# A new order for the first quarter of a hand-written work list and of the list of loads

## The chip, the cores and the metric

The kernel runs on one core of one Trainium2 chip. The metric is the device time of one execution in microseconds: 364.95 us, the median of three runs before the change (364.71 to 365.18).

## The reference, cut to what matters

Causal attention with 16 extra "beacon" keys that every query sees, then a gated feed-forward block on its output:

```python
# q, k, v: 8 batches, 8 heads, 576 rows, 64 columns;  beacon_k, beacon_v: 16 rows
k_all = concat([beacon_k, k]);  v_all = concat([beacon_v, v])
scores = q @ k_all.T / 8, causal mask on the 576 ordinary keys
a = softmax(scores);  attn = a @ v_all
x = attn.transpose(0, 2, 1, 3).reshape(4608, 512)
g = x @ w_gate                      # 512 to 1536
out = (g * sigmoid(g) * (x @ w_val)) @ w_out
```

All inputs are float32 in memory; the kernel casts them to bf16 in the load.

## The kernel before, in words

**Attention.** Heads are worked in pairs, 4 pairs to a batch. Queries and keys have to be turned (head dimension onto partitions) first: of batch 0 in five turns from the loaded runs, of batches 1 and 2 one turn to a pair (`turn`, letter T) after the two heads were laid side by side by `pair_up` (g on VectorE, f on GpSimd), of batches 3 to 7 by DMA transposes (t). `turned_copy` brings them to SBUF (K and Q on VectorE, k and q on ScalarE). A pair's scores are four units A to D (`scores`: S, or s with the mask added by matmuls; letters below such as "scores 2.1B" are batch 2, pair 1, unit B), each with one exponent (`exponent`, E, ScalarE) and for S a mask after it (D on VectorE, M on GpSimd). The product with v has two halves (`pv`, P and p) and a division (`normalize`, R). In batch 0 the first 240 queries of all pairs go ahead: `pv_front` (Z), `normalize_front` (N), `x_turn_front` (J), `x_copy_front` (I); the rest of its rows are turned by X and copied by y. Later batches use DMA transposes (V).

**Feed-forward.** 9 chunks of 512 tokens by 12 column tiles. `gate_value` has two halves (G, H), `tanh` (a, ScalarE) and two VectorE steps (1, 2) follow; `project` (F) is one twelfth of half an output tile, O and o evacuate and store. Chunk 0 starts with its first 240 tokens, so the first gate product waits only for the front rows of batch 0.

**Weights in two shapes.** Scores, turns of batch 1 and 2, gate, value and projection use 64 rows of the array at a time, two such products side by side. `pv` of batches 0 to 3, `pv_front` and the x turns use all 128 rows.

**PSUM.** There are 4 slots of two banks for everything (`take`, `give`): a unit that takes a slot waits for the step that gave that slot back. Slots go round in program order.

**The order.** Every engine works in the order in which the letters of `plan` stand. Each letter l starts the next load of `order_of_loads`, on GpSimd's queue. The first 24 of them are free; each later one waits for the last but one PE step placed before it (line 739, "paced load"). GpSimd has eight completion semaphores for its loads, so a load also waits until the load eight places before it has landed. Names of loads: K0.0 and Q0.4 are keys and queries of batch 0, heads 0 to 3 or 4 to 7; K1, Q2 are a whole batch; v0.0 is the beacons of v, v0.1 to v0.5 are blocks of rows of v of batch 0 (block by block of 128 keys); g0 to g4 and u0 to u4 are column parts of w_gate and w_val (1, 2, 3, 3 and 3 tiles); b1, b2 are beacon keys; o0, o1 are the halves of w_out; k3.1 is a block of rows of k of batch 3.

**Warmers.** Letter h makes the next scores, pv or pv_front issue two more 64 x 128 matmuls of the identity before its own, into the slot that it then overwrites (`keep_warm`, line 182).

Of the kernel before, what the change touches and what calls it, by code (L numbers as in the profile page):

```python
# [16 lines left out]
S = 576  # L17
D = 64
# [68 lines left out]
def kernel(  # L87
# [579 lines left out]
    def select_below():  # L667
        for row in range(2):
            r = slice(HALF * row, HALF * row + HALF)
            nc.gpsimd.affine_select(  # L670
                out=below[r], in_=below[r], compare_op=ALU.is_ge, fill=-30000.0, base=0,
                pattern=[[HALF, 2], [-1, P]], channel_multiplier=1,
            )

    def select_upper():
        nc.gpsimd.affine_select(
            out=upper[:], in_=upper[:], compare_op=ALU.is_ge, fill=0.0, base=0, pattern=[[1, P + NB]],
            channel_multiplier=-1,
        )
# [38 lines left out]
        named[f"K0.{h}"] = lambda h=h: runs(0, k, h, h + 4, FRONT, ROWS)  # L718
        named[f"Q0.{h}"] = lambda h=h: runs(0, q, h, h + 4, FRONT, ROWS)
    order_of_loads = """  # L720
    K0.0 Q0.0 v0.2 Q0.4 K0.4 v0.1 v0.0 v0.3 v0.4 v0.5 g1 u0 g0 u1 g2 u2 K1 Q1 b1 u3 g3 g4 u4 Q2 v1.5 K2 v1.3 v1.2
    v1.0 v1.1 v1.4 b2 o0 o1 v2.2 k3.0 v2.1 q3.2 v2.5 k3.5 v2.4 v2.3 v2.0 q3.4 q3.0 q4.2 k4.0 v3.3 k3.1 q4.0 k3.4
    k3.2 q3.1 v3.0 k4.2 q3.3 k4.3 v3.5 q4.4 k3.3 v3.4 v3.2 k4.5 k4.1 q4.3 q4.1 v4.1 v4.5 v4.3 v4.0 k4.4 v3.1 v4.2
    q6.1 k5.0 q5.1 q5.4 k5.3 k5.5 k6.0 k5.2 k5.1 q5.0 k6.2 q5.3 v4.4 k6.1 q6.0 q6.2 k6.5 q5.2 v5.2 k5.4 k7.0 k7.2
    v5.5 q7.1 k6.3 k7.1 v5.1 q7.2 k7.4 q7.3 q6.3 v5.4 k6.4 q6.4 k7.5 v5.0 k7.3 v5.3 q7.4 q7.0 v6.0 v6.1 v6.2 v6.4
    v6.3 v6.5 v7.4 v7.5 v7.2 v7.1 v7.3 v7.0
    """
    loads = [named[name] for name in order_of_loads.split()]
    assert sorted(order_of_loads.split()) == sorted(named)
    turns = [load for b in range(NPE, B) for load in dma_transposes(b)]  # L730

    def piece(kind):
        as_kind = {"s": "S", "M": "D", "k": "K", "q": "Q", "Y": "y", "o": "O", "i": "I", "A": "e", "f": "g"}.get(kind, kind)
        n = done.get(as_kind, 0)
        done[as_kind] = n + 1
        if kind == "l":
            if n >= FREE_LOADS:

                after(nc.gpsimd.nop(), passed[-2], "paced load")
            loads[n]()  # L740
        elif kind == "b":
            cast_beacons()
        elif kind == "W":
            first_beacon_turn()
        elif kind in "Ae":
            first_beacon_copy(nc.vector if kind == "A" else nc.scalar)
        elif kind == "0":
            regroup()
        elif kind in "gf":
            pair_up(n, nc.vector if kind == "g" else nc.gpsimd)  # L750
        elif kind == "B":
            select_below()
        elif kind == "U":
            select_upper()
        elif kind == "T":
            turn(n)
        elif kind in "KkQq":
            turned_copy(n, kind in "Kk", nc.vector if kind in "KQ" else nc.scalar)
        elif kind in "Ss":
            scores(n, kind == "s")  # L760
        elif kind == "E":
            exponent(n)
        elif kind in "DM":
            while shown[n + skipped[0]][1]:
                skipped[0] += 1
            mask(n + skipped[0], nc.vector if kind == "D" else nc.gpsimd)
        elif kind in "Pp":
            pv(n, kind == "p")
        elif kind == "R":
            normalize(n)  # L770
        elif kind == "X":
            x_turn(n)
        elif kind in "Yy":
            x_copy(n, nc.vector if kind == "Y" else nc.scalar)
        elif kind == "V":
            x_transpose(n + 1)
        elif kind == "t":
            turns[n]()
        elif kind in "GH":
            gate_value(n, kind == "H")  # L780
        elif kind == "Z":
            pv_front(n)
        elif kind == "N":
            normalize_front(n)
        elif kind == "J":
            x_turn_front(n)
        elif kind in "Ii":
# [39 lines left out]
    for kind in "".join(plan.split()):  # L827
# [8 lines left out]
        S=16 * B, E=16 * B, P=NP, p=NP, R=NP, X=NPAIR, y=NPAIR, V=B - 1, t=len(turns), G=NU, H=NU, Z=2, N=2, J=2, I=2, a=NU, **{"0": 1, "b": 1, "W": 1, "e": 1, "g": NPAIR * (NPE - 1), "B": 1, "U": 1, "1": NU, "2": NU}, F=2 * NF * 2 * NCH, O=4 * NCH + 2, T=len(TURNS),  # L836
        K=len(COPIES), Q=len(COPIES),  l=len(loads),
# [31 lines left out]
```

## Time and profile before

| | us |
|---|---|
| median of three runs | 364.95 |
| span of the profiled execution, first to last instruction | 362.0 |
| the rest of the median, outside that span | 2.95 |
| PE busy in the span | 352.9 (97%) |
| VectorE, ScalarE, GpSimd busy | 225.4, 187.6, 124.6 |

PE means TensorE matmuls, POOL is GpSimd, DVE is VectorE, ACT is ScalarE. The trace has the start and length of every instruction, what ended the idle time before it, and when each load landed. A busy PE is not always a PE at its full rate, since the ends of pipelined matmuls are modelled: a matmul of 128 rows by 65 columns is shown with 0.19 us while the next one starts 0.03 us later.

### The profile page before, as it was taken

What the parts mean: (1) busy time and instruction counts of PE and PEld (TensorE: products, weight loads), DVE (VectorE), ACT (ScalarE), POOL (GpSimd) and SP (SyncE); (2) the same over time, 40 slices, a digit from 0 to 9 for tenths busy, and PEclk for the clock granted to TensorE, in tenths of its full rate; (3) what the DMA queues carried; (4) which work ended last, traced back from release to release, by engine and by line L of the source; (5) the groups of instructions that cost most, each with busy time, mean ns of one, the idle gap of its engine ahead of it and who ended that gap; (6) DMA issues with size and microseconds to landing.
All of it is one profiled execution on the core that took longest, in us unless ns stands there. A gap on an engine that the chain in (4) does not pass through costs nothing.

```text
span 362.0 us, 11888 instructions
## 1 busy us (share of the span) xinstructions
PE 352.9 (97%) x5160; PEld 198.6 (55%) x5160; DVE 225.4 (62%) x439; ACT 187.6 (52%) x284; POOL 124.6 (34%) x188
## 2 busy tenths in 40 slices
PE   7799999999999999999999999999999999999996
PEld 3587565654444566554565566546655554455544
DVE  5577997566766654487528754776467764464342
ACT  4966999723434777544863576447633232221310
POOL 8945499926247545374423013111000000000000
PEclk9999999999999999999999999999999999999999
DMA  8999999999999999999979829502413000110113
GB/s 121 156 197 204 191 191 158 174 175 147 149 147 121 134 136 129 153 174 135 122 132 147 109 37 154 67 6 26 113 62 65 2 2 0 61 60 1 61 60 116
DMA packets 146132, 39.74 MB, mean 110 GB/s; under 512 B 131488, under 2 KB 141728, under 8 KB 146080
## 3 DMA queue, kind: packets, MB, share of 16 engines
q0 software_dynamic: 97424, 19.00, 72.1%
q1 hardware_dynamic: 48368, 19.79, 27.9%
q8 instruction: 40, 0.66, 0.8%
q10 hardware_dynamic: 288, 0.20, 0.2%
q14 instruction: 12, 0.10, 0.1%
HBM read 38.27 MB, written 9.44 MB: 132 GB/s over the span
## 4 chain that ended last, share of the span: by engine, by line
PE 85%; DMA 5%; POOL 5%; DVE 2%; ACT 1%; issue 1%; POOLq 0%
PE gv_ps L168 49%; PE o_ps L168 25%; DMA qk<-in_q_dram 5%; PE s_ps L168 5%; PE pv_ps L168 4%; PE pv_ps L493 2%; POOL qk L209 2%; POOL vb L219 1%; DVE x L522 1%; POOL wg L248 1%; POOL wv L248 1%; DVE p L414 1%; PE t_ps L166 0%; ACT p L405 0%; ACT th L579 0%
## 5 line engine op out<-in xcount | busy, mean ns | idle before, releaser
L168 PE MATMUL gv_ps<-xT,wv 64*128 64x512 bf16 (+2 forms) x912 | 203.2, 365 | 0.0
L168 PE MATMUL gv_ps<-xT,wg 64*128 64x512 bf16 (+2 forms) x912 | 202.8, 365 | 0.1
L579 ACT ACTIVATE th<-gv_ps 128x512 f32<-128x512 f32 (+2 forms) x114 | 65.4, 575 | 116.5 <-PE gv_ps L168 116.1
L405 ACT ACTIVATE p<-s_ps 128x832 bf16<-128x832 f32 (+2 forms) x127 | 104.3, 868 | 32.4 <-PE s_ps L168 28.7
L168 PE MATMUL o_ps<-wo,hT 64*128 64x512 bf16 (+2 forms) x912 | 116.5, 365 | 0.2
L584 DVE SCALAR_TENSOR_TENSOR u<-th,gv_ps 128x512 f32<-128x512 f32 (+2 forms) x114 | 74.7, 656 | 65.9 <-ACT th L579 65.1
L168 PEld LDWEIGHTS <-wg 64*128 64x128 bf16 x912 | 82.5, 94 | 45.9 <-PE gv_ps L168 2.4
L168 PEld LDWEIGHTS <-wv 64*128 64x128 bf16 x912 | 81.8, 94 | 40.1 <-issue 0.7
L591 DVE SCALAR_TENSOR_TENSOR hT<-gv_ps,u 128x512 bf16<-128x512 f32 (+2 forms) x114 | 74.7, 661 | 3.0
L168 PEld LDWEIGHTS <-hT 64*128 64x128 bf16 x912 | 42.3, 94 | 34.1 <-PE o_ps L168 1.2
L219 POOL DMA_DIRECT2D vb<-in_v_dram x40 | 33.9, 853 | 64.1 <-PE s_ps L168 25.7
L168 PE MATMUL s_ps<-qT,kT 64*128 64x336 bf16 (+3 forms) x512 | 43.0, 250 | 1.9 <-ACT kT L256 1.0
L168 PEld LDWEIGHTS <-kT 64*128 64x128 bf16 x512 | 23.8, 94 | 22.9 <-ACT kT L256 1.8
L219 POOL DMA_DIRECT2D qk<-in_q_dram x25 | 21.2, 851 | 25.7 <-PE gv_ps L168 7.1
L414 DVE TENSOR_TENSOR p<-p,upper 128x256 bf16<-128x256 bf16 (+2 forms) x84 | 24.0, 317 | 9.8 <-ACT p L405 8.1
L522 DVE TENSOR_TENSOR x<-pv_ps,rec 128x640 bf16<-128x640 f32 (+1 forms) x32 | 25.3, 791 | 1.2
L521 DVE RECIPROCAL rec<-pv_ps 128x10 f32<-128x10 f32 (+1 forms) x32 | 6.8, 213 | 28.1 <-PE pv_ps L168 22.7
L258 DVE COPY o_sb<-o_ps 128x512 f32<-128x512 f32 (+2 forms) x20 | 12.7, 654 | 17.0 <-PE o_ps L168 13.9
L219 POOL DMA_DIRECT2D qk<-in_k_dram x25 | 21.3, 856 | 5.4 <-PE gv_ps L168 4.3
L418 POOL TENSOR_SCALAR_AFFINE_SELECT p<-p 128x256 bf16<-128x256 bf16 (+2 forms) x46 | 17.4, 399 | 14.0 <-ACT p L405 13.8
L168 PEld LDWEIGHTS <-p 64*128 64x128 bf16 x960 | 18.8, 94 | 4.5 <-PE pv_ps L168 0.2
L168 PE MATMUL pv_ps<-vb,p 64*128 64x65 bf16 x960 | 19.9, 189 | 0.0
(65 smaller groups left out, 141.4 us busy)
## 6 DMA issues: line engine op xcount, KB each, us to landing
out_dram<-o_sb SPq DMA_DIRECT2D x34, 256.0 KB, 2.6
vb<-in_v_dram POOLq DMA_DIRECT2D x24, 128.0 KB, 5.7
qk<-in_q_dram POOLq DMA_DIRECT2D x21, 128.0 KB, 5.6
qk<-in_k_dram POOLq DMA_DIRECT2D x16, 128.0 KB, 5.9
wo<-in_moe_w_out_dram POOLq DMA_DIRECT2D x2, 768.0 KB, 10.1
wg<-in_moe_w_gate_dram POOLq DMA_DIRECT2D x3, 384.0 KB, 11.7
wv<-in_moe_w_val_dram POOLq DMA_DIRECT2D x3, 384.0 KB, 14.2
qk<-in_k_dram POOLq DMA_DIRECT2D x2, 576.0 KB, 11.5
```

The lines of the kernel that those rows point to most:

```text
L168: ins = nc.tensor.matmul(o, lhsT=l, rhs=r, start=start, stop=stop)
L209: return nc.gpsimd.dma_start(qk[b % 2][base : base + HALF, RUN * h0 : RUN * h1] .rearrange("p (h e) -> p h e", e=RUN)[:, :, D * i0 : D * i ...
L219: return nc.gpsimd.dma_start(dst[p0 : p0 + n, c, :, 0:D], src[b, :, r : r + n, :].rearrange("h j d -> j h d"))
L248: nc.gpsimd.dma_start(t[:, :, cols], src[:, cols].rearrange("(kk p) f -> p kk f", p=P))
L258: eng.tensor_copy(o, i)
L405: nc.scalar.activation(p_of(b, m, u == "A")[:, :, c0 : c0 + w], ps[:, :, 0:w], ACT.Exp, scale=0.125)
L414: nc.vector.tensor_tensor(out=ap, in0=ap, in1=upper[:, None, d : d + w].to_broadcast([P, 2, w]), op=ALU.mult)
L418: nc.gpsimd.affine_select(out=ap, in_=ap, compare_op=ALU.is_ge, fill=0.0, base=d, pattern=[[0, 2], [1, w]], channel_multiplier=-1,)
L522: nc.vector.tensor_tensor(out=xs[b][:, c0:NKT, P * m : P * m + P].rearrange("p c (h d) -> p h c d", d=D), in0=o[:, :, :, 0:D], in1=rec[:, ...
L579: nc.scalar.activation(th[:, 0:w], gvs[n][:, 0, 0:w], ACT.Tanh, scale=0.5)
L584: nc.vector.scalar_tensor_tensor(out=u[:, 0:w], in0=ths[n][:, 0:w], scalar=1.0, in1=gvs[n][:, 0, 0:w], op0=ALU.add, op1=ALU.mult)
L591: nc.vector.scalar_tensor_tensor(out=hTs[j][:, f, c0:c1], in0=gvs.pop(n)[:, 1, 0 : c1 - c0], scalar=0.5, in1=ths.pop(n)[:, 0 : c1 - c0], o ...
```

## The change

Three things are done. The first 708 of the 1756 letters of the plan stand in a new order, and the first 59 of the 125 loads. The rule for pacing is spelled by letter: L is a free load, l a paced one; there are again 24 free loads, but the 23rd (v1.3) is paced and the 28th (Q2) is free. Five of the ten warmers move from the first stretch to the end of the new part, just before half p of pv 3.1; they are issued by the next P, of pv 3.2. Nothing is added or removed.

The set of the first 16 loads is the same, as is that of the first 32; K1 and Q1 stay number 17 and 18, o0 and o1 number 33 and 34. Within the first 16, u1 goes ahead of all of v0 but v0.2, and g0 ahead of v0.5.

```diff
     order_of_loads = """
-    K0.0 Q0.0 v0.2 Q0.4 K0.4 v0.1 v0.0 v0.3 v0.4 v0.5 g1 u0 g0 u1 g2 u2 K1 Q1 b1 u3 g3 g4 u4 Q2 v1.5 K2 v1.3 v1.2
-    v1.0 v1.1 v1.4 b2 o0 o1 v2.2 k3.0 v2.1 q3.2 v2.5 k3.5 v2.4 v2.3 v2.0 q3.4 q3.0 q4.2 k4.0 v3.3 k3.1 q4.0 k3.4
+    Q0.0 K0.0 Q0.4 K0.4 v0.2 u1 v0.0 v0.1 v0.4 v0.3 g0 v0.5 g1 u0 g2 u2 K1 Q1 b1 g3 u3 u4 v1.3 g4 v1.0 K2 v1.1
+    Q2 v1.4 v1.5 b2 v1.2 o0 o1 k3.1 v2.3 q4.0 v2.2 v2.1 v2.5 v2.4 k3.0 v2.0 v3.5 q4.2 k4.2 q3.0 k3.2 k3.4 k3.5
...
     def piece(kind):
...
-        if kind == "l":
-            if n >= FREE_LOADS:
-
+        if kind in "lL":
+            if kind == "l":
                 after(nc.gpsimd.nop(), passed[-2], "paced load")
             loads[n]()
...
     plan = """
-    0lhbTqllhhWKeBhTQslTlEKlsqlkElhhSlTQsKElKEslssUQEshsEhDElshEEEllhlTQZkNZsNSPpJEEIlsJPllERIpSXlDR
-    PpSyEGXRHElDSylDGaElGH1H2aaXD1lf2Py1pGGlH2GRaXHlylH12aaGGH112a2HG1G2Haa1HaTq2lgGl1H2k1GaS21l2HSE
-    alsElGS12ETHgKQGEaS12lEHlTDa1GSqH2glDkESfaGslE1H2ElSEMDlTGMSQaKEHSMM12aGEs1HEa2T1qPpMllkDPfllSpR
-    E2sRfsPDpSEEFEFFSFRDFFlSElSPEMpTFFlFERkFSfFFlqDSSFFFlEDFDEFSFTEFDFFFSQVlEkEFFDDFFOSEOllFFTtFqKFD
-    lMSFESFFFFElSSMDlFElPplPlpERsFDFRFFFEFStlFFEGSGHtFDHDEaGMF1FFaH12POlOpaPp2RlG1GlRHtal2G1HHGVa21l
+    0bTLWeLBTTqKQKhsLLLLsELqkELTLhSsQKsLELEEKsLQTELsshsUEQkEDhZhsEEZLNNsJSLIJLEsPIEpESPpRXSEDRPypDS
+    LGERXEDHGyaLXD1PpH2yGLaGRLLl1HXHa2LGyfaGH12Ga1H2a1H21a2l1GGHa21H2GGaH1aTH2qgGalH11kS22TalGE12KLS
+    HEDsQalSEGSgD12EHTGEaqSglHlk1S2lElaGE1sl2lHMElSafD1GE2MlSHSETEGQasK1HEMTaMM2PqpS1ks2ERPEDspflSEP
+    EfDpRlFFFRSlDESEFFlTFPpSkMqflRFFVFDFFFllTSFFFFEFlQESkFFFSSFFFFEEDFSFEFFOESDFFDFlSFEFDOTSEDqKlDFF
+    llFPlElPlpSFEFFpFMMRFFFRSsltEFFDllFEDFSGGlESFHOEOaHDPt1aGllD1pMHt2GRP2patlH1aRGl2G1HHGVa21lll2lt
...
```

From the 60th load (k3.3, between gate product 22 and gate product 23) on the order is the old one again, but for the five h at the end of the new part.

## Rows read from the trace of the kernel before

**Rows 1.** The page, busy us of PE and its weight loads, of all instructions:
```profile
PE 352.9 (97%) x5160; PEld 198.6 (55%) x5160; DVE 225.4 (62%) x439; ACT 187.6 (52%) x284; POOL 124.6 (34%) x188
```
**Rows 2.** By stage, busy us and count of PE, PEld, DVE, ACT, POOL; then clock:
```profile
0.00:10.00 10.00, 7.27 (x154) 3.94 (x158) 4.88 (x21) 4.77 (x10) 8.76 (x19) 1.00 0.98 126
10.00:20.00 10.00, 7.99 (x238) 6.24 (x224) 6.24 (x18) 9.30 (x13) 9.91 (x15) 1.00 1.67 158
```
**Rows 3.** PE in order of time, to 35 us: start, length, group [idle before, releaser]:
```profile
7.53 0.45 PE L166 MATMUL t_ps<-ident,qk 64*64 64x64 bf16 x32
15.03 0.95 PE L437 MATMUL pvf_ps<-vb,p 128*128 128x65 bf16 x18
...
17.39 0.90 PE L493 MATMUL pv_ps<-vb,p 128*128 128x65 bf16 x24
...
21.52 0.26 PE L168 MATMUL gv_ps<-xT,wg 64*128 64x240 bf16 x1
...
32.55 0.44 PE L166 MATMUL t_ps<-ident,side 64*128 64x64 bf16 x18 [0.22 <-POOL side L258]
```
**Rows 4.** POOL in order of time, at the first pair_up:
```profile
31.35 1.14 POOL L258 COPY side<-qk 128x1152 bf16<-128x1152 bf16 x1 [7.37 <-DMA qk<-in_q_dram]
```
**Rows 5.** One load at a time, v0.1, v0.5, u0: its issue, then time to landing:
```profile
L219 POOL DMA_DIRECT2D vb<-in_v_dram x1: 861/861/861, 8.4 to 8.4; - x1
...
DMA to landing us min/median/max: 6.2/6.2/6.2
...
L219 POOL DMA_DIRECT2D vb<-in_v_dram x1: 792/792/792, 11.5 to 11.5; - x1
...
DMA to landing us min/median/max: 5.0/5.0/5.0
...
L248 POOL DMA_DIRECT2D wv<-in_moe_w_val_dram x1: 757/757/757, 13.4 to 13.4; - x1
...
DMA to landing us min/median/max: 5.2/5.2/5.2
```
**Rows 6.** ACT in order of time:
```profile
7.64 0.78 ACT L405 ACTIVATE p<-s_ps 128x736 bf16<-128x736 f32 x1 [1.34 <-PE s_ps L168]
8.32 0.59 ACT L256 ACTIVATE qT<-t_ps 128x512 bf16<-128x512 bf16 x1
...
11.54 4.80 ACT L405 ACTIVATE p<-s_ps 128x832 bf16<-128x832 f32 x6
16.18 0.77 ACT L256 ACTIVATE kT<-t_ps 128x640 bf16<-128x640 bf16 x1
```
**Rows 7.** PE in order of time, into a stretch of pv and out of it:
```profile
76.94 0.38 PE L168 MATMUL gv_ps<-xT,wv 64*128 64x512 bf16 x1
77.16 0.38 PE L168 MATMUL gv_ps<-xT,wv 64*128 64x512 bf16 x1
77.47 1.99 PE L493 MATMUL pv_ps<-vb,p 128*128 128x65 bf16 x60
79.09 0.37 PE L493 MATMUL pv_ps<-vb,p 128*128 128x65 bf16 x7
79.39 0.39 PE L168 MATMUL gv_ps<-xT,wg 64*128 64x512 bf16 x1
```
**Rows 8.** PE in order of time, from pv 1.0 to pv 1.3:
```profile
49.65 1.35 PE L493 MATMUL pv_ps<-vb,p 128*128 128x65 bf16 x39
51.22 0.36 PE L493 MATMUL pv_ps<-vb,p 128*128 128x65 bf16 x6 [0.22 <-POOL p L418]
...
56.55 1.08 PE L493 MATMUL pv_ps<-vb,p 128*128 128x65 bf16 x30
```
**Rows 9.** PE in order of time, two groups of warmers:
```profile
6.22 0.40 PE L182 MATMUL s_ps<-ident 64*128 64x128 bf16 x8
...
8.47 0.29 PE L182 MATMUL s_ps<-ident 64*128 64x128 bf16 x4
```
**Rows 10.** PE at its start and at its end, and the clock of the last 2 us:
```profile
1.53 3.96 PE L685 MATMUL idle_ps<-p 128*128 128x512 bf16 x12 [1.53 <-DVE p L656]
...
357.79 0.75 PE L168 MATMUL o_ps<-wo,hT 64*128 64x128 bf16 x20
...
360.00:362.00 2.00, 0.00 (x0) 0.00 (x0) 0.00 (x0) 0.00 (x0) 0.00 (x0) 0.57 0.10 27
```

More of the change, by code (lines that the diff above doesn't have):

```diff
@@ L50 @@
 W_PARTS = [(0, 1), (1, 3), (3, 6), (6, 9), (9, 12)]
-FREE_LOADS = 24
 NHT = 2
@@ L720 @@
     order_of_loads = """
-    K0.0 Q0.0 v0.2 Q0.4 K0.4 v0.1 v0.0 v0.3 v0.4 v0.5 g1 u0 g0 u1 g2 u2 K1 Q1 b1 u3 g3 g4 u4 Q2 v1.5 K2 v1.3 v1.2
-    v1.0 v1.1 v1.4 b2 o0 o1 v2.2 k3.0 v2.1 q3.2 v2.5 k3.5 v2.4 v2.3 v2.0 q3.4 q3.0 q4.2 k4.0 v3.3 k3.1 q4.0 k3.4
[L723 to L726, printed above, removed]
+    Q0.0 K0.0 Q0.4 K0.4 v0.2 u1 v0.0 v0.1 v0.4 v0.3 g0 v0.5 g1 u0 g2 u2 K1 Q1 b1 g3 u3 u4 v1.3 g4 v1.0 K2 v1.1
+    Q2 v1.4 v1.5 b2 v1.2 o0 o1 k3.1 v2.3 q4.0 v2.2 v2.1 v2.5 v2.4 k3.0 v2.0 v3.5 q4.2 k4.2 q3.0 k3.2 k3.4 k3.5
+    q3.4 v3.0 q3.1 q4.4 q3.2 q3.3 v3.3 k4.0 k4.3 k3.3 v3.4 v3.2 k4.5 k4.1 q4.3 q4.1 v4.1 v4.5 v4.3 v4.0 k4.4
+    v3.1 v4.2 q6.1 k5.0 q5.1 q5.4 k5.3 k5.5 k6.0 k5.2 k5.1 q5.0 k6.2 q5.3 v4.4 k6.1 q6.0 q6.2 k6.5 q5.2 v5.2
+    k5.4 k7.0 k7.2 v5.5 q7.1 k6.3 k7.1 v5.1 q7.2 k7.4 q7.3 q6.3 v5.4 k6.4 q6.4 k7.5 v5.0 k7.3 v5.3 q7.4 q7.0
+    v6.0 v6.1 v6.2 v6.4 v6.3 v6.5 v7.4 v7.5 v7.2 v7.1 v7.3 v7.0
     """
@@ L732, in piece @@
     def piece(kind):
-        as_kind = {"s": "S", "M": "D", "k": "K", "q": "Q", "Y": "y", "o": "O", "i": "I", "A": "e", "f": "g"}.get(kind, kind)
+        as_kind = {"s": "S", "M": "D", "k": "K", "q": "Q", "Y": "y", "o": "O", "i": "I", "A": "e", "f": "g", "L": "l"}.get(kind, kind)
         n = done.get(as_kind, 0)
         done[as_kind] = n + 1
-        if kind == "l":
-            if n >= FREE_LOADS:
+        if kind in "lL":
+            if kind == "l":
                 after(nc.gpsimd.nop(), passed[-2], "paced load")
@@ L806 @@
     plan = """
-    0lhbTqllhhWKeBhTQslTlEKlsqlkElhhSlTQsKElKEslssUQEshsEhDElshEEEllhlTQZkNZsNSPpJEEIlsJPllERIpSXlDR
-    PpSyEGXRHElDSylDGaElGH1H2aaXD1lf2Py1pGGlH2GRaXHlylH12aaGGH112a2HG1G2Haa1HaTq2lgGl1H2k1GaS21l2HSE
-    alsElGS12ETHgKQGEaS12lEHlTDa1GSqH2glDkESfaGslE1H2ElSEMDlTGMSQaKEHSMM12aGEs1HEa2T1qPpMllkDPfllSpR
-    E2sRfsPDpSEEFEFFSFRDFFlSElSPEMpTFFlFERkFSfFFlqDSSFFFlEDFDEFSFTEFDFFFSQVlEkEFFDDFFOSEOllFFTtFqKFD
-    lMSFESFFFFElSSMDlFElPplPlpERsFDFRFFFEFStlFFEGSGHtFDHDEaGMF1FFaH12POlOpaPp2RlG1GlRHtal2G1HHGVa21l
-    ll2ltGHal1G2lGHHa1aatlt21tGH1H2lattF2aGFH112FF2FFGSaEFlHt1GFFaHa2Gltl1t2GtlH12latH12Fa12FFGGtDHS
-    ltlaE1FHFFaG2lSFHtl12allF12GFElMFllFHaSG1FEFHaGFFolMHl2l1G2aSOF1H2FaE1FtFG2sHFEaFslF1FDFlSE2FDFE
-    DFSESlPpFFFRlDFFFlStFESSDFFEFFsEDFOPEpMPEOpSFFlFRMStRFEFEFSsFEMEFFDFFPplFSFFFFFlFRDSSEFEtFtSFDFF
+    0bTLWeLBTTqKQKhsLLLLsELqkELTLhSsQKsLELEEKsLQTELsshsUEQkEDhZhsEEZLNNsJLSLIJLEsPIEpESPpRXSEDRPypDS
+    LGERXEDHGyaLXD1PpH2yGLaGRLLl1HXHa2LGyfaGH12Ga1H2a1H21a2l1GGHa21H2GGaH1aTH2qgGalH11kS22TalGE12KLS
+    HEDsQalSEGSgD12EHTGEaqSglHlk1S2lElaGE1sl2lHMElSafD1GE2MlSHSETEGQasK1HEMTaMM2PqpS1ks2ERPEDspflSEP
+    EfDpRlFFFRSlDESEFFlTFPpSkMqflRFFVFDFFFllTSFFFFEFlQESkFFFSSFFFFEEDFSFEFFOESDFFDFlSFEFDOTSEDqKlDFF
+    llFPlElPlpSFEFFpFMMRFFFRSsltEFFDllFEDFSGGlESFHOEOaHDPt1aGllD1pMHt2GRP2patlH1aRGl2G1HHGVa21lll2lt
+    GHal1G2lGHHa1aatlt21tGH1H2lattF2aGFH112FF2FFGSaEFlHt1GFFaHa2Gltl1t2GtlH12latH12Fa12FFGGtDHSltlaE
+    1FHFFaG2lSFHtl12allF12GFElMFllFHaSG1FEFHaGFFolMHl2l1G2aSOF1H2FaE1FtFG2sHFEaFslF1FDFlSE2FDFEDFSES
+    lPpFFFRlDFFFlStFESSDFFEFFsEDFOPhhhhhEpMPEOpSFFlFRMStRFEFEFSsFEMEFFDFFPplFSFFFFFlFRDSSEFEtFtSFDFF
     FFFEEFlVFFsoOElFFSFtFFDFtSMPEDEtSFElpSDRFFMFFtlMPtESSFEEpRFttFFGFDDSEGHFGa12HHlla1aG21FHl2aGlFHl
```

## The prediction, made before the result was known

> **What bounds the kernel now.** I read the page first: PE is busy in 352.9 of 362.0 us [rows 1]. Then the busy time by stage: PE has 7.27 us of the first ten and 7.99 of the second, while ACT fills 9.30 and POOL 9.91 of that second stage [rows 2]; so the idle time of PE that a new order could use is some 4.7 us in 20, of which 1.53 lie ahead of the first matmul [rows 10] and stay. After 21 us PE waits hardly at all: 0.22 us at turn 5, the first of batch 1 [rows 3], and 0.22 in pv 1.1 [rows 8], so everything late is paid to the end. Then PE in order of time with the waits, and behind each wait the queue that ended it. Turn 5 started at 32.55, after the copy of the side, which POOL began at 31.35 when Q1 had landed [rows 3, 4]. Loads in front of that point land one behind another: v0.1 was issued at 8.43 and landed 6.2 later, at 14.6; v0.5 at 11.54 + 5.0 = 16.5; u0 at 13.4 + 5.2 = 18.6 [rows 5]. So three things order the first 33 us: the row of loads, ACT's sixteen exponents of 0.80 us (six took 4.80 [rows 6]), and PE's own order.
>
> The sum is made against the profiled span, 362.0; the median of the runs, 364.95, is 2.95 more, launch and end, which the change doesn't touch. About 0.2% (0.73 us) is what a measurement of this kernel can tell from no change.
>
> **A. To the first gate product: +0.5 us (0 to +1.1).** pv_front 0 needs v0.0, v0.1, v0.2; the end of each half of pv 0.0 needs v0.5. Before, pv_front 0 began at 15.03 and pv 0.0 at 17.39 [rows 3], close behind their loads. In the new list u1 stands ahead of v0.0 and v0.1, and g0 and u1 ahead of v0.5. In bf16 the first runs are 384 KB, the rest of K0 and Q0 640, v0 592, g1 or u1 256, g0 or u0 128. Through v0.1 the new order has loaded 1536 KB, what the old one had only at its ninth load, between v0.1 (14.6) and v0.5 (16.5): I take 15.8 (15.2 to 16.4). Through v0.5 it has 2000 KB, exactly what the old one had through u0, which landed at 18.6 [rows 5]; I take 18.5.
>
> In the new order all three front turns stand ahead of scores 0; the third ran at 7.53 before [rows 3], behind scores 0, and can't be earlier than its queries. So the first exponent starts at about 8.2, not 7.64 [rows 6]; two copies of 0.5 and 0.6 follow, the exponents 1 to 6 run to about 14.4, the key copy of turn 4 (0.77 [rows 6]) now stands ahead of exponent 7 and not behind 9, and exponent 8 ends at 16.6. Behind pv_front 0, which waits for v0.1, PE has scores 9, pv_front 1 and scores 10 queued, and ACT's exponent 9 waits for scores 9: 15.8 + 0.4 + 0.4, so exponent 9 runs 16.7 to 17.5. Its slot goes to x_turn_front 0 (17.5); the division of pv_front 1 ends at 18.1, x_turn_front 1, scores 12 follow, and pv 0.0 starts at 18.8, 1.4 late, but with 0.9 us of work done that stood behind it before (scores 12, the two front x turns). From there PE is the limit: pv 0.0, 0.1, 0.2 at 0.8 each (0.90 shown [rows 3], the last end modelled), scores 13, 14, 15 and an x turn make 3.4: the first gate product at 22.2 against 21.52 [rows 3], one unit of scores (0.2) further on. That is +0.5.
>
> **B. Warmers: +0.28 us (0.2 to 0.4).** Eight showed 0.40, four 0.29 [rows 9], 0.028 a matmul. Ten that stood in the idle first stretch are now issued with pv 3.2, where PE waits for nothing: 10 x 0.028.
>
> **C. Turn 5 and behind it: -0.3 us (-0.4 to +0.2).** Q1 keeps its place in the row, so it lands at 31.2 still and its side is ready at 32.5. PE was there at 32.33 and now gets there at 32.33 + 0.5 + 0.46 = 33.3, since half G of gate product 10 (four pairs of 272 columns) now stands ahead of the turn: the wait of 0.22 is gone, with some 0.1 of start-up. What is late next is scores 16, which needs the key copy: ACT now has a tanh between the query copy and the key copy, PE has half H of gate product 11 to cover it. Both come out at 2.0 us from turn to scores 16.
>
> **D. 36 to 49 us: +0.1 us (0 to +0.4).** Turn 7 takes the slot of gate product 12, and DVE now has two copies of turn 6, a pair_up and two masks ahead of the step that frees it; followed step by step it comes out 0.2 behind PE, half of which I put down to rounding.
>
> **E. pv 1.0 to pv 1.3: -0.5 us (-0.8 to 0).** Before, 49.65 to 56.55 [rows 8]. The POOL mask for which pv 1.1 waited 0.22 now stands ahead of a second pair_up and comes some 1.5 us before it is needed; the exponents stand a little earlier among the scores. On the other side pv 1.1 is split off by two units of scores. Followed step by step the stretch takes 6.4 and not 6.9.
>
> **F. Splitting pv of batch 2: +0.45 us (+0.2 to +0.7).** Into a stretch of pv PE pays 0.31 between the last gate matmul and the first of pv, against 0.22 from gate to gate: 0.09. Out of it, the last seven pv take 0.30 to the next gate matmul, at the mean of 0.032 of the sixty that is 0.08 too much [rows 7]. A visit so costs some 0.17 to 0.19 beyond its work. pv 2.0 and 2.1 were one stretch on PE and are two; pv 2.2 and 2.3 were one and are three, with gate and value products between the halves. Three visits more are 0.55, less 0.1 for small waits that the products between them fill.
>
> The row shows this with no rule needed: 0.31 against 0.22. The Trainium skill (TensorEngine Tiling (Array Packing), Key Properties) says that changing the tiling mode drains the TensorE, while changing the tile does not; the trace agrees, 0.09 in and 0.08 out. By that rule the 14 more changes of the whole new part would give 14 x 0.09 = 1.2 us; by the rows of PE's idle time six of them fall in the first 20 us, where PE waits anyway, and I count eight at most (E has two).
>
> At equal cost, because their sets don't change: K1, Q1, o0, o1 keep their rank in the row of loads, and the row is full (POOL issues far ahead of landing), so they land when they did. Q2 goes from 24th to 28th and lands some 4 us later, at 46.5; its pair_up starts when POOL is past v2.3, at 47.5, for turn 9 at about 49.5: covered by 0.8 us, and this much plus what Q2 is later is the price if it isn't. The 20 DMA transposes and the first x transposes on SP's queue move by a few steps, the latter earlier, and nothing on PE stands close behind them. The pacing is a wait for a PE step two back, which POOL meets long after it was met, because the eight semaphores hold it longer.
>
> **Sum:** 0.5 + 0.28 - 0.3 + 0.1 - 0.5 + 0.45 = +0.53. Span 362.5, time 365.5.
>
> **Rivals.**
> 1. *The new order gains (364.0).* v0.1 lands by 15.2 and v0.5 by 18: A is +0.1, C -0.4, D 0, E -0.8, F +0.2, and 0.4 of small late starts between 57 and 77 goes too; with B that is -1.0. For it: ACT is the limit of the second ten microseconds, at 9.30, and the new order leaves it no gap from 9.8 to 17.5. Against it: the bytes ahead of v0.1. It decides at A below +0.2.
> 2. *Batch 0's v is later still (366.4).* v0.1 at 16.4 and v0.5 at 19.1, pv 0.0 at 19.4: A is +1.1, and D +0.4: 365.5 + 0.6 + 0.3. For it: an 0.4 us error in the landing of one load is 0.4 us at the end.
> 3. *Q1 absorbs it (365.0).* PE is early at turn 5 in both orders and waits there for a side at 32.5: A and C cancel, B, D, E, F stay: +0.3, or nothing. Against it: half G of gate product 10 ahead of the turn fills the wait.
> 4. *The clock falls (367.2).* PE at the start needs 3.96 us for 4608 columns, 1.16 columns a ns, the 1.2 GHz level; the clock showed 0.57 in the last two microseconds, after PE had ended at 358.5 [rows 10]. The new order has five warmers fewer and, by A, a stretch of 1.4 us without a matmul ahead of pv_front 0. Should the clock fall there, some 4 us as at the start would run at half rate: up to +1.8. Against it: before, waits in this stage kept the clock at 1.00 [rows 2], though they were shorter.
>
> That the change doesn't do what it says has no room: the letters and names are the same multisets.
>
> **The numbers.** Forecast, as summed: 0.45; rival 1: 0.22; rival 2: 0.18; rival 3: 0.10; rival 4: 0.05. The forecast's own range, 364.9 to 366.2, lies two thirds within 0.73 of the old time and one third above: same 0.30 + 0.10 (rival 3), slower 0.15 + 0.18 + 0.05, faster 0.22. The range for 8 in 10 takes in rivals 1 to 3: 363.8 to 366.9.
>
> **What would show it.** A: pv_front 0 starting at 15.5 or later, with a load of v as what ended PE's wait, and the first gate product at 22 or later. If that stands at 21.7 or before, rival 1 holds. B: ten identity matmuls ahead of pv 3.2 and no wait around them. C: turn 5 without a wait, its side ready before. D: a wait at turn 7 that DVE ends. E: no POOL wait in pv 1.1. F: one step of 0.3 us at the start of each of pv 2.0, 2.1, 2.2 and 2.3. Rival 4: the granted clock below 1.00 between 14 and 25 us. The prediction is wrong if PE's lag over the old order at the same work, at gate product 18 (71 us), is outside -0.7 to +1.6.

## The result, and the profile after

The changed kernel takes 367.26 us (median of 4 executions, 366.72 to 367.87) against 365.06 for the kernel before beside it: 1.0061 times as long, 95% interval 1.0047 to 1.0076. That is 2.2 us slower, above the range of 363.8 to 366.9. The profiled execution took 367.87 us with a span of 366.0; what lies around the span is 1.87 us here. Other executions of the kernel before, timed later with their spans, have 1.8 us around spans of 362.1 to 365.7, so the profile of before, at 362.0, is that of a quick one, and its 2.95 us to the median was not launch and end alone.

PE by stage in the profile after: busy time and count, granted clock, DMA's share, GB/s (the answers to [rows 2], of PE alone):

```profile
0.00:10.00 10.00, 6.28 (x106) 0.97 0.87 124
10.00:20.00 10.00, 9.31 (x194) 0.52 1.79 164
50.00:60.00 10.00, 8.72 (x204) 1.00 1.50 181
```

In the first ten PE does less than before (6.28 us, it was 7.27). In the second ten it is busier than it was (9.31, it was 7.99) and yet no further: the granted clock is 0.52 where it was 1.00. It fell from 2.4 to 1.2 GHz at 9.40 us and was back at 19.64. And ten microseconds at 50 us have lost 1.28.

PE in order of time in the profile after, the answers to [rows 3] with the new waits, and behind them one line of before, scores of 336 columns:

```profile
7.11 0.44 PE L165 MATMUL t_ps<-ident,qk 64*64 64x64 bf16 x31 [0.53 <-DMA qk<-in_q_dram]
8.06 0.28 PE L167 MATMUL s_ps<-ident,below 64*128 64x48 bf16 x8
10.17 0.75 PE L165 MATMUL t_ps<-ident,qk 64*64 64x64 bf16 x40 [1.83 <-DMA qk<-in_k_dram]
12.32 0.57 PE L167 MATMUL s_ps<-qT,kT 64*128 64x336 bf16 x4
16.07 0.84 PE L436 MATMUL pvf_ps<-vb,p 128*128 128x65 bf16 x12 [0.43 <-DMA vb<-in_v_dram]
20.55 0.90 PE L492 MATMUL pv_ps<-vb,p 128*128 128x65 bf16 x24
23.97 0.26 PE L167 MATMUL gv_ps<-xT,wg 64*128 64x240 bf16 x1
34.87 0.43 PE L165 MATMUL t_ps<-ident,side 64*128 64x64 bf16 x18
57.72 0.82 PE L167 MATMUL o_ps<-wo,hT 64*128 64x512 bf16 x6 [1.03 <-issue]
70.34 1.13 PE L492 MATMUL pv_ps<-vb,p 128*128 128x65 bf16 x30 [0.25 <-DVE kT L257]
134.86 0.45 PE L181 MATMUL pv_ps<-ident 64*128 64x128 bf16 x10
```
```profile
12.03 0.35 PE L168 MATMUL s_ps<-qT,kT 64*128 64x336 bf16 x4
```

Turn 3 (turns are numbered from 0; turns 0 to 2 are the front ones) now stands ahead of scores 2 and waits until 10.17 for K0.0; the clock falls inside that wait, and scores of 336 columns, four in 0.35 us before, take 0.57. pv_front 0 and pv 0.0 come 1.0 and 3.2 us late, the first gate product at 23.97 (21.52 in [rows 3]). Turn 5 has lost its wait. At 57.72 stands a wait that nothing in the profile ends ("issue"), and at 70.34 a new one behind a key copy.

### The profile page after: what moved, and what is told of

Read it like the earlier page. It is cut to its first block, busy times and chain, and to the rows that moved or that the text cites. A ratio compares the mean times of both kernels' runs of the same rounds, so it can differ in the third digit from the quotient of the medians.

```text
span 366.0 us, 11890 instructions
## 1 busy us (share of the span) xinstructions
PE 356.5 (97%) x5160; PEld 201.2 (55%) x5160; DVE 224.0 (61%) x439; ACT 187.8 (51%) x284; POOL 125.1 (34%) x188
## 4 chain that ended last, share of the span: by engine, by line
PE 92%; POOL 2%; ACT 2%; DMA 2%; issue 1%; DVE 0%; POOLq 0%
PE gv_ps L167 52%; PE o_ps L167 24%; PE s_ps L167 6%; PE pv_ps L167 4%; PE pv_ps L492 4%; DMA vb<-in_v_dram 2%; POOL qk L208 1%; ACT p L404 1%; PE t_ps L165 0%; PE pvf_ps L436 0%; POOL vb L218 0%; ACT qT L255 0%; ACT kT L255 0%; PE xt_ps L535 0%; PE xf_ps L467 0%
## 5 line engine op out<-in xcount | busy, mean ns | idle before, releaser
L167 PE MATMUL s_ps<-qT,kT 64*128 64x336 bf16 (+3 forms) x512 | 44.2, 259 | 0.3 <-ACT kT L255 0.3
L413 DVE TENSOR_TENSOR p<-p,upper 128x256 bf16<-128x256 bf16 (+2 forms) x84 | 22.3, 297 | 6.3 <-ACT p L404 5.4
```

The lines of the kernel that those rows point to most:

```text
L167: ins = nc.tensor.matmul(o, lhsT=l, rhs=r, start=start, stop=stop)
L413: nc.vector.tensor_tensor(out=ap, in0=ap, in1=upper[:, None, d : d + w].to_broadcast([P, 2, w]), op=ALU.mult)
```

## The experiments

The work list and the list of loads can be cut where both kernels have done the same work, and joined anew; most kernels here are such joins. "Early" is up to the second gate product, "middle" from there to product 9 of the first projection (58 us), "end" what follows to pv of batch 3. Ratios are to the kernel before on the same chip, with the 95% interval. "Lag" is how much later PE starts its next matmul, at the same amount of matmul work done (warmers counted), in one profile than in another. Most diffs are told in words or shortened; a letter with a number is that step of the list, counted from 0.

**Two joins at the second gate product.** x1_early_before:

```diff
 to the second gate product: before's work list and loads
-then before's
+then after's, without hhhhh
```

> The work list and the loads up to the second gate product are those of before (ten early warmers), the rest those of after, without the five late warmers. Theory 1 (the wait of turn 3 for K0.0 at 8.2 us drops the clock to 1.2 GHz for 10 us, and the early part owes 2.5 us to it): no such wait, clock 1.0 all through, and the time comes to 364.8 to 365.6. Theory 2 (the order of the early loads makes the lag, the clock none of it): the same here, 364.8 to 365.6. Theory 3 (the loss is made later: wo's later landing and the instruction stall at projection 0.0, the extra visits of pv, 0.8 + 0.6): 366.2 to 367.

Measured: 367.18 us, 1.0062 (1.0039 to 1.0084). x2_early_after:

```diff
-to the second gate product: before's
+to the second gate product: after's
 then before's
+hhhhh behind pv 3.1
```

> The reverse: after's work list and loads up to the second gate product, then before's, with the five late warmers kept after pv 3.1. Theory 1 and theory 2: the early 2.5 us are here, 366.8 to 367.6. Theory 3: 365.0 to 365.8, as the later loss is gone.

Measured: 365.73, 1.0020 (0.9999 to 1.0042). Theory 3 holds (x1 is 0.2 us above its range) and 1 and 2 seem to fall: the late parts alone make the whole loss, the early part 0.7 us with the warmers. That was read too early, as z1 shows below.

**The clock kept up, and turn 3 behind scores 2.** x3_kept_warm:

```diff
-0bTLWeLBTTqKQKhsLLLLsELqkEL
+0bTLWeLBTTqKQKhsLLLLhhhhhhhhhhhhhhhhhhhhhhhhhhsELqkEL
```

> After, with 26 more warmers (52 matmuls of 128 columns on the identity) ahead of scores 1, so that TensorE has work while turn 3 waits for K0.0. Theory 1: the granted clock stays at 2.4 GHz and most of the early lag goes: 365.2 to 366.2. Theory 2: the clock stays up too but v0.1 and v0.5 and K0.0 land as late, and the time stays at 366.8 to 367.4. Theory 3: 366.8 to 367.4.

Measured: 368.48, 1.0112 (1.0077 to 1.0147): slower than after. PE in its profile:

```profile
7.87 1.61 PE L181 MATMUL s_ps<-ident 64*128 64x128 bf16 x52
9.69 0.51 PE L165 MATMUL t_ps<-ident,qk 64*64 64x64 bf16 x40
12.61 0.17 PE L167 MATMUL s_ps<-ident,below 64*128 64x16 bf16 x1 [1.16 <-issue]
13.96 0.36 PE L167 MATMUL s_ps<-qT,kT 64*128 64x336 bf16 x4
60.75 1.24 PE L167 MATMUL o_ps<-wo,hT 64*128 64x512 bf16 x9 [0.72 <-issue]
```

The warmers keep the clock up, as theory 1 says: scores of 336 columns take 0.36 us. But only part of the early loss goes: the first gate product stands at 23.22 (23.97 in after, 21.52 in [rows 3]). Two waits of the kind "issue" are new, at 12.61 and 60.75 (see below), and this profile is the quickest of its executions (367.47; the slowest 371.25). What the others lost stays open. x4_turn3_behind:

```diff
-    0bTLWeLBTTqKQKhsLLLLsELqkELTLhSsQKsLELEEKsLQTELsshsUEQkEDhZhsEEZLNNsJLSLIJLEsPIEpESPpRXSEDRPypDS
+    0bTLWeLBTTqKQKhsLLLLsELqkELLhSTsQKsLELEEKsLQTELsshsUEQkEDhZhsEEZLNNsJLSLIJLEsPIEpESPpRXSEDRPypDS
```

> After, with turn 3 behind scores 2 instead of ahead of it. Theory 1: scores 2 fills 0.3 us of the wait and its exponential starts at 9.7 instead of 11.5; the clock may still fall, as 1.5 us of the wait are left; with the fall 366.5 to 367.2, without it 365.2 to 366.2. Theory 2: pv_front 0 still waits for v0.1 at 16.0, so 366.8 to 367.4. Theory 3: 366.8 to 367.4.

Measured: 367.70, 1.0077 (1.0047 to 1.0106): no gain. Scores 2 then waits for its key copy, 1.25 us, and the clock is low from 7.7 to 14.5 us instead.

**What "issue" waits for.** PE's products in the profiles of x1 and x4, and the DMA queues from 51 to 54 us in before and from 54 to 57 us in after (packets, MB, the time they took as a share of 16 engines' time):

```profile
54.89 0.78 PE L492 MATMUL pv_ps<-vb,p 128*128 128x65 bf16 x20
56.70 0.47 PE L492 MATMUL pv_ps<-vb,p 128*128 128x65 bf16 x10 [1.03 <-issue]
```
```profile
57.14 0.82 PE L167 MATMUL o_ps<-wo,hT 64*128 64x512 bf16 x6 [0.97 <-ACT p L404]
```
```profile
q8 instruction: 1, 0.02, 2.0%
```
```profile
q8 instruction: 1, 0.02, 1.9%
```

In x1 the wait cuts a pv in two; in after and x4 it stands ahead of the first product. Counted from the start, it is the same place in all three, whatever instruction stands there: the 991st pair of weight load and matmul. The page of after has 40 packets of 16 KB on queue q8, "instruction", for 5160 pairs, so one for some 128. The seventh ran at 55.5 to 56.4 us in after, 54.4 to 55.3 in x1 and 51.6 to 52.6 in before; in no profile of this study does that pair start less than 1.3 us behind the packet's end, and in fifteen of twenty it starts 1.3 to 1.5 behind it, before's among them. From 90 to 120 us most packets start within a microsecond of the pair 128 ahead of their own; at 50 us the seventh starts 2.7 to 3.1 us after pair 863 in before's order (1.0 in z1) and 3.4 to 4.1 in after's, where PE does not stop in between. From pair 863 to 991 before takes 5.2 us, 2.9 to the packet's start, 1.0 for it and 1.3 behind it; after takes 6.2, as the packet starts 1.1 later. The shortest here is 4.7 (z1).

That instructions are what "issue" waits for is read from these places. Every wait of that kind above 0.15 us in the twenty profiles stands at pair 224, 991 or 1118, within one place of 223, 991 and 1119, which are multiples of 128 apart. In x3, with 52 more pairs in front, one comes at 12.61, 1.5 us behind the end of a packet (10.23 to 11.13). Why the packet starts later in after's order isn't shown.

**The parts behind the cut.** x5_end_after:

```diff
 to product 9 of the first projection: before's
-then before's
+then after's, without hhhhh
```

> Before up to product 9 of the first projection (about 58 us), then after's order and loads, without the five late warmers. If the +2.0 us of x1_early_before lies in the wait of 1.0 us ahead of the 991st pair of weight load and matmul (at 56.7 us), where the same pair waits in after and in x4 whatever instruction it is (theory A: instructions are fetched 128 pairs at a time, and that fetch ran at 54.4 to 55.3 us instead of 51.6): this kernel is at 365.2 to 365.6. If it lies in the cutting up of batch 2's pv (theory B, term F of the prediction, and the later loads): 365.9 to 366.6.

Measured: 365.77, 1.0023 (1.0006 to 1.0040): between the two theories, nearer to B. x6_middle_after:

```diff
 to the second gate product: before's
-to product 9 of the first projection: before's
+to product 9 of the first projection: after's
 then before's
```

> After's order and loads only from the second gate product to product 9 of the first projection (22 to 58 us), before's ahead of it and behind it. Theory A: 366.2 to 366.9, with a wait of about 1 us ahead of pair 991 and the fetch before it at 54 us or later. Theory B: 365.0 to 365.6, with no such wait or one made up for later.

Measured: 366.15, 1.0044 (1.0025 to 1.0063), the wait ahead of pair 991 0.45 us, its packet at 53.5: theory A's wait at half its size. x7_middle_order:

```diff
 x6_middle_after
-after's loads in the middle
+before's loads in the middle, at the same share of the work
```

> As x6_middle_after, but with before's loads in before's places: only the order of the work is after's in that stretch. Theory A with the order of the loads as what delays the fetch: no wait at pair 991, 365.0 to 365.6. Theory A with the denser work as what uses the instructions up sooner: the wait stays, 366.0 to 366.9. Theory B: 365.0 to 365.6.

Measured: 366.86, 1.0054 (1.0031 to 1.0076), with no wait at pair 991 but 0.78 us at turn 9 for its side. A miss for all three. x8_turn5_after:

```diff
 to the second gate product: before's
-to turn 6: before's
+to turn 6: after's
 then before's
```

> After's order and loads only from the second gate product to turn 5 (22 to 34 us). The prediction's term C had turn 5's wait at -0.3; the lag of after against before fell by 0.68 us there. If nothing takes it back: 364.4 to 364.9. If the loads of batch 2 that come later for it do: 365.0 to 365.6.

Measured: 365.56, 1.0011 (0.9997 to 1.0025): taken back. Its profile shows 0.35 us of wait in pv 0.3 at 24.8, which stands too close behind its exponent when nothing ahead of it is late; x1 and x6 have the same, after has not.

**Four more.** b0_before_again has no edit.

> Before, unchanged, for a second profile of it. The first had a span of 362.0 us, while other executions of it had 362.5 to 364.3; so this one should be near 363, with about 1 us more of waits somewhere in the first 60 us, and if the early clock matters little, with a clock of 0.995 like most of the others.

Measured: 365.36, span 363.6, the clock low from 9.2 to 16.0 us, and the expected loss of 1.0 us. PE, then POOL:

```profile
51.47 1.20 PE L493 MATMUL pv_ps<-vb,p 128*128 128x65 bf16 x34 [0.46 <-POOL p L418]
52.92 0.35 PE L493 MATMUL pv_ps<-vb,p 128*128 128x65 bf16 x6 [0.25 <-POOL p L418]
```
```profile
49.58 0.87 POOL L219 DMA_DIRECT2D vb<-in_v_dram  x1
50.44 0.54 POOL L219 DMA_DIRECT2D qk<-in_beacon_k_dram  x1
50.98 0.43 POOL L418 TENSOR_SCALAR_AFFINE_SELECT p<-p 128x256 bf16<-128x256 bf16 x1
51.34 0.84 POOL L219 DMA_DIRECT2D vb<-in_v_dram  x1
52.17 1.65 POOL L418 TENSOR_SCALAR_AFFINE_SELECT p<-p 128x160 bf16<-128x160 bf16 x5
```

Three loads that are needed much later are issued by POOL between the masks that pv 1.0 and 1.1 need, 2.25 us in all. x9_turn5_only:

```diff
-... H9 a9 T5 q6 act2(7) l g1 G10 ...
+... H9 a9 act2(7) G10 T5 q6 l g1 ...
```

(act2(7) is step 2 of gate product 7.)

> Before, with the first half of gate product 10 ahead of turn 5 and nothing else moved (step 18 of the gate value ahead of Q6 with it). If the wait of turn 5 for its side is what made the lag fall by 0.65 us in after: 364.2 to 364.7. If PE's time there is taken back by the next loads: no change, 364.7 to 365.3.

Measured: 365.07, 1.0003 (0.9989 to 1.0017). Turn 5's wait went (the lag falls by 0.64 there), 0.71 came back in the next two microseconds of work. x10_pv21_behind:

```diff
-F35 P8 E42 P9 l p8 S43
+F35 P8 E42 l p8 P9 S43
```

> x5_end_after with pv 2.1's first half behind the second half of pv 2.0. In after and x5 pv 2.1 waited 0.4 us at 70.3 and 68.8, for the key copy of turn 12, which frees its PSUM slot. Theory C (that wait is 0.4 of term F's 1.0): the wait is gone and the time 0.3 to 0.4 less than x5's 365.8. If the visits alone make F: 365.6 to 366.0, as x5.

Measured: 364.90, 0.9998 (0.9981 to 1.0016), 0.25% less than x5. In the profile the wait is gone: the lag rises by 0.65 from 65 to 80 us, in x5 by 1.08. x11_wo_in_thirds:

```diff
-        fs = slice(6 * i, 6 * i + 6)
-        nc.gpsimd.dma_start(wo[:, fs, :], ...)
+        for f in range(6 * i, 6 * i + 6, 2):
+            fs = slice(f, f + 2)
+            nc.gpsimd.dma_start(wo[:, fs, :], ...)
```

> After, with each of the two loads of wo (768 KB) issued as three of 256 KB. Theory A, with the instruction fetch held up on its ring by the load in progress: the seventh fetch starts less than 3 us after the 863rd pair (3.9 in after), the wait ahead of pair 991 is under 0.3 us, and the time 366.2 to 366.8. If the fetch waits by bytes in front of it whatever their pieces: 367.0 to 367.6.

Measured: 370.54, 1.0153 (1.0138 to 1.0168), above both forecasts. The seventh packet started 3.8 us after pair 863, as in after: smaller pieces don't let it through sooner. The price is elsewhere: four more issues on POOL stand ahead of the side of turn 9, and PE waits for it, 2.24 us at 54.5; behind that wait the clock is low from 56.0 to 59.4.

**Four with before's spread in mind.** y0_after_again has no edit to after.

> After, unchanged, on the same chip as the pieces, for its spread and a second profile: 366.5 to 367.5 (+0.6% as before). If the pieces add up (early +0.7, middle +1.6 or less, end +0.8), it is at +2.2 to +3.1 us.

Measured: 367.17, 1.0054 (1.0036 to 1.0072). y1_after_pv21 is after with the edit of x10.

> After with pv 2.1's first half behind the second half of pv 2.0, as x10 has it. Theory C: the wait of 0.4 us for turn 12's PSUM slot at 70 us is gone and the time is 0.3 to 0.9 us under y0 (x10 was 0.9 under x5, where 0.4 was expected). If the slack is used up elsewhere: as y0.

Measured: 367.01, 1.0051 (1.0033 to 1.0069). The wait is gone from the profile (0.44 us of lag less than y0 there); the times can't tell 0.4 us. y2_middle_clean:

```diff
-x6_middle_after, cut at the second gate product
+the same, cut at the second half of gate product 5
```

> Before up to the second half of gate product 5 (28 us), after's order and loads to product 9 of the first projection, then before's. Cut later than x6_middle_after, so that pv 0.3 stays where before has it: in x6, x1 and x8 it stood too early for its exponent (0.87 us of lag at 24 us) and in after it did not. If that cut made half of x6's +1.6: 365.3 to 366.0. If the middle itself makes it (the wait ahead of pair 991): 366.0 to 366.6.

Measured: 366.11, 1.0038 (1.0012 to 1.0063). Its profile has another cause than either theory. PE, then POOL:

```profile
52.01 0.44 PE L165 MATMUL t_ps<-ident,side 64*128 64x64 bf16 x18 [1.82 <-POOL side L257]
```
```profile
48.73 0.83 POOL L218 DMA_DIRECT2D qk<-in_k_dram  x1 [0.50 <-issue]
49.56 0.42 POOL L417 TENSOR_SCALAR_AFFINE_SELECT p<-p 128x256 bf16<-128x256 bf16 x1
49.92 0.88 POOL L218 DMA_DIRECT2D vb<-in_v_dram  x1
50.80 1.16 POOL L257 COPY side<-qk 128x1152 bf16<-128x1152 bf16 x1
```

Q2 had landed at 43.0, but in after's order POOL issues k3.1 and v2.3 ahead of the side; PE, which is not late here, meets turn 9 before it. Behind the wait the clock is low from 53.8 to 57.2 us. y3_masks_first:

```diff
 on POOL, before's order
-mask 7, v2.2, k3.0, v2.1, mask 9 to 12
+mask 7, mask 9 to 12, v2.2, k3.0, v2.1
```

> Before, with the loads v2.2, k3.0 and v2.1 behind the five POOL masks of batch 1 (they stood between them, 2.2 us of POOL's time). In the second profile of before, pv 1.1 waited 0.46 and 0.25 us for those masks at 51 to 53 us, and the lag rose by 1.0 us there, which after avoids (term E). If most executions of before pay that: 364.0 to 364.6. If only that one did: 364.6 to 365.1.

Measured: 363.61 us, 0.9961 (0.9944 to 0.9978), all but one of its twelve executions between 363.37 and 363.86. It beats both kernels and both forecasts. The masks run in one row and pv follows without a wait for them:

```profile
49.41 2.00 POOL L417 TENSOR_SCALAR_AFFINE_SELECT p<-p 128x256 bf16<-128x256 bf16 x6
```
```profile
50.67 1.54 PE L492 MATMUL pv_ps<-vb,p 128*128 128x65 bf16 x45
```

So the loads between the masks cost most executions of before, some 1.6 us by the times (the one profile that shows the loss has 1.0), and its spread comes from there.

**Two on y3.** z1_early_on_y3:

```diff
-to the second gate product: before's
+to the second gate product: after's
 then y3_masks_first's
+hhhhh behind pv 3.1
```

> After's order and loads up to the second gate product, then those of y3_masks_first, with the five late warmers: the early part and term B alone, on the kernel that no longer waits for the masks and whose executions lie within 0.4 us. By the profiles the early part of after costs 1.3 to 2.2 us at 34 us against y3's: 365.2 to 366.1 with the warmers. By x2 against before (+0.7): 364.2 to 364.6. Where the granted clock stays at 1.0, the first should hold less of it if theory 1 has any part.

Measured: 366.84, 1.0042 (1.0018 to 1.0066) of before, 3.2 us over y3 (3.0 by the ratios): above both forecasts, and not all of it early. At 49 us its profile has a wait of its own; VectorE, GpSimd, then PE:

```profile
45.56 2.09 DVE L413 TENSOR_TENSOR p<-p,upper 128x160 bf16<-128x160 bf16 x1
```
```profile
46.04 1.16 POOL L257 COPY side<-qk 128x1152 bf16<-128x1152 bf16 x1
```
```profile
49.03 0.44 PE L165 MATMUL t_ps<-ident,side 64*128 64x64 bf16 x18 [1.49 <-DVE hT L590]
```

The mask, 0.23 us otherwise, runs until GpSimd's copy of a side is done, and what VectorE does behind it comes late; its step for turn 8's slot is what PE waits for. z2_end_on_y3:

```diff
 to product 9 of the first projection: y3_masks_first's
-then y3_masks_first's
+then after's, without hhhhh
```

> y3_masks_first up to product 9 of the first projection, then after's order and loads without the late warmers: term F alone. Three more visits of pv at 0.19 us and 0.4 us of wait for turn 12's PSUM slot: +0.9 to +1.0, 364.5 to 364.8. Visits alone, as the prediction had it: +0.45 to +0.6, 364.0 to 364.3.

Measured: 365.20, 1.0010 (0.9994 to 1.0025) of before, 1.6 us over y3 (1.8 by the ratios): above both forecasts. Its profile, the quickest of its executions (364.1), has no wait for turn 12's slot, but 0.39 us at 65.7 for another slot, which an evacuation of the projection frees.

## Why the prediction was wrong

PE's lag over the profile of y3, which has neither the wait for masks nor a low clock, worked out from the matmul records of each trace, in us:

```
PE at            first    turn 5   ahead of    behind   ahead of    behind pv   end
                 gates    passed   proj. 0     its 1st  pv 2.0      of batch 2
before, first    -0.4     -0.6     -0.6        -0.7     -0.2        -0.2        -0.2
before, second    0.6      0.1      0.1         0.9      1.4         1.4         1.4
after             2.2      1.3      2.0         2.9      2.9         3.9         4.0
y0 (after)        3.1      2.2      3.0         3.5      3.5         4.5         4.7
x3 (kept warm)   -0.3     -0.9     -0.3        -0.2      1.0         1.9         2.7
z1 (early)        2.8      2.3      4.0         3.4      3.5         3.5         3.7
z2 (end)         -0.4     -0.4     -0.4        -0.7     -0.8         0.4         0.3
```

(The columns are 10, 22, 36, 40, 50, 64 and 336 us of matmul work; y3's executions are as quick as the quickest of before. x3's row counts its 52 added products as work done, so it flatters x3: its span is 3.6 us above y3's.) The prediction named -0.7 to +1.6 as the lag over before's first profile at gate product 18 that it could live with; at that work (56 us) it is some 3.7.

**A failed: +0.5 (0 to +1.1) was forecast over before's first profile, 2.6 (after) and 3.5 (y0) came.** The step took the loads of v as what sets the early part, and there it was near: v0.1 ended a wait of 0.43 at 16.07, forecast 15.8. What it put at nothing was the clock, which falls behind waits of the turns. It knew that the third front turn "can't be earlier than its queries", and gave turn 3 no wait at all; but the new list asks for Q0.0 ahead of K0.0, which landed at 10.12 (8.65 in before's first profile), and PE stood 1.83 us for it. Then rival 4 happened, at 9.4 us and not ahead of pv_front 0, for ten microseconds and not four.

The wait for K0.0 is not the whole of it. In y0 the clock fell at 8.03, ahead of that wait and behind two waits of the third front turn, and the scores at 8.08 are slow already:

```profile
6.62 0.21 PE L165 MATMUL t_ps<-ident,qk 64*64 64x64 bf16 x1 [0.61 <-DMA qk<-in_k_dram]
7.34 0.44 PE L165 MATMUL t_ps<-ident,qk 64*64 64x64 bf16 x31 [0.51 <-DMA qk<-in_q_dram]
8.08 0.49 PE L167 MATMUL s_ps<-qT,kT 64*128 64x240 bf16 x4
9.69 0.75 PE L165 MATMUL t_ps<-ident,qk 64*64 64x64 bf16 x40 [0.92 <-DMA qk<-in_k_dram]
```

In z1 and x4 it fell at 7.9 and 7.7, behind 1.2 and 1.4 us of such waits. Which wait makes it fall stays open. In the new order it was low for 6.8 to 13.7 us in every profile that shows its start but x3's, where it stayed up, in the old for 0 to 6.8. By how long the clock was low ahead of 22 us, the start of the first gate product (us; x2, whose trace doesn't show the fall, left out):

| low for | before's early order | after's early order |
|---|---|---|
| not at all | 21.5 to 22.0 (3 profiles) | 23.2 (x3) |
| 3.4 | 22.0 to 22.4 (7) | |
| 6.8 | 22.6 (2) | 23.4 (x4) |
| 10.2 | | 23.8 to 24.6 (3) |
| 13.7 | | 24.7 to 24.9 (2) |

Down either column a microsecond at the low level goes with 0.13 to 0.2 us; by that estimate the clock is 1.3 to 2.0 of after's 2.45, and the rest, 0.4 to 1.1, is about what A forecast. x3 agrees as far as it goes: less its wait of 1.16 for the instructions that its own warmers used up, its first gate product would stand at 22.1 by estimate, and A had 22.2.

The times of single executions say the same. Of z1's twelve, the six with a mean granted clock of 0.986 or less took 366.9 to 368.6 us (median 367.5), the other six 364.4 to 366.8 (365.4). Of the sixteen of after and y0, the five at 0.986 or less have a median of 367.9, the others of 366.9. So the clock is a part of the loss and not the whole.

Rival 4's time, 367.2, was met by luck: it priced four low microseconds and not ten, and the rest of its sum was off as well. Its chance of 0.05 was too small: the argument that before's waits kept the clock at 1.00 [rows 2] rested on one execution, and the second profile of before has it at 0.70 there. Of the twelve profiles with before's early order nine show it low. (Rival 3's own terms add up to 0.33, so its time is 365.3 and not 365.0.)

**B was right:** ten products in 0.45 us at 134.86, and the lag rises by 0.27 there.

**C was right and worth nothing.** Turn 5 lost its wait; the lag falls by 0.84 and rises by 0.42 in the next four microseconds of work. x9, that edit alone, gains nothing that can be measured.

**D and the equal costs failed in part.** 26 to 36 us of work cost 0.3, forecast 0.1. "They land when they did" was wrong of wo: o0 landed at 55.1 and not 52.8. POOL stood 3.02 us up to 44.2 for a PE step, so the pacing, a wait that by the prediction POOL would find long met, did hold the loads up. That did not stop PE: the wait ahead of projection 0, 1.03 us in the profile, was at pair 991, for instructions by the reading above, a term that the sum did not have. It raised the lag by 0.9 us in after and 0.5 in y0. Q2's side, called covered by 0.8 us, was not: POOL began it at 50.0 and not 47.5, y2 waits 1.82 for it, and after escapes, by 0.2 us, only because PE comes late itself.

**E was right, and before paid more for it than its profile showed:** -0.5 forecast from 0.22 of wait [rows 8]; the second profile of before lost 1.0 at that place, and y3, which only brings those masks forward, gains 1.6 in time. After has no wait for those masks either, and lies 3.6 above y3 and 2.0 above before.

**F was mis-sized: +0.45 (0.2 to 0.7) forecast, 1.0 in the profiles of after and y0, 1.2 in z2.** The three visits cost what the step said. Into and out of one of them in after:

```profile
78.85 0.38 PE L167 MATMUL gv_ps<-xT,wv 64*128 64x512 bf16 x1
79.16 0.63 PE L492 MATMUL pv_ps<-vb,p 128*128 128x65 bf16 x15
```

0.31 from start to start, against 0.21 from gate to gate, and 0.09 out: 0.19 each, 0.57 in all; x10 has 0.65. What failed is "less 0.1 for small waits": pv 2.1 takes the PSUM slot that turn 12's key copy frees, and comes 0.4 us late for it (the row at 70.34 has 0.25, as ends are modelled). In z2 a wait for another slot, 0.39 us, is in its place.

**The sum.** By the times of z1 and z2, the early part with the warmers and the end would bring y3's 363.6 to 368.4 with nothing for the fetch; after has 367.2. The intervals of these times are 0.6 to 0.9 us to either side, so that the parts don't add is likely and not shown. What is seen is that later waits change with PE's lateness. In x2's profile pv 1.0 and 1.1 have no wait for masks, as PE comes late, but scores wait for a key copy:

```profile
50.66 0.37 PE L167 MATMUL s_ps<-qT,kT 64*128 64x336 bf16 x4 [0.86 <-DVE kT L257]
```

Its lag over the second profile of before rises from 2.2 to 3.4 there and falls back to 2.4 as before waits for its masks. And z1 is no quicker than x2 (1.0042 and 1.0020, the intervals overlap), though it has the quick masks of y3; its wait of 1.49 us at 49 us stands against them. So neither 0.7 nor 3.2 is the early part's own price.

Open: why x3's other executions were slower than its profiled one, and why x10 gained 0.9 us in time where its profile shows 0.4 (the two intervals overlap).

## What to carry to other kernels

Before a step is moved in a list of work, look up the landing of every input of the step, the first row asked for included, and what the granted clock does behind a stall there, in more than one execution. Look at a joined kernel's own new waits before its time is called the price of a part: a wait for something that comes at a time of its own hides lateness ahead of it, and lateness can make new waits. Loads that nobody needs soon did better behind the masks on POOL's queue than between them (y3).

## What the runs showed of the hardware

TensorE's instructions come in packets of 16 KB on a DMA queue, one for some 128 pairs of weight load and matmul, and from 90 to 120 us the next one starts when PE is about 128 pairs ahead of its first. At 50 us, with loads in flight, it starts 2.7 to 4.1 us later (1.0 in z1), and the pair runs 1.3 us or more behind its end. The stretch of pv at 50 us can use 128 up in some 5 us, and PE then waits with nothing in the profile that ends the wait. Smaller loads in the queue did not help (x11).

A mask on VectorE that meets GpSimd's copy of a side lasts beyond the copy's end: of 51 such meetings in the twenty profiles, 46 masks end 0.1 to 0.5 us behind it, and took up to 2.09 us. Masks that meet none have a median of 0.28.

A granted clock of 1.00 ahead of a trace's first record of it is no evidence. The profile of x2 has this for its second ten microseconds, and these scores in it:

```profile
10.00:20.00 10.00, 8.49 (x178) 1.00 1.77 158
```
```profile
11.77 0.57 PE L167 MATMUL s_ps<-qT,kT 64*128 64x336 bf16 x4
```

0.57 us for four products of 336 columns is what after took at 1.2 GHz; 0.35 is the time at 2.4. The first record of that trace is at 21.0 us.
